# A retention layer with two GLU-like blocks: raw weight pieces requested two conversions ahead, q scaled one slot earlier, the second stage's first inputs loaded and split in the first

## Chip, core and metric

One core of one Trainium2 chip. The metric is device time in microseconds (us) for one launch of the whole computation; lower is better. The engines are TensorE (PE, matmuls; PEld is its weight load), VectorE (DVE), ScalarE (ACT), GpSimd (POOL) and the queue that issues DMAs, SyncE (SP). Each engine runs its own list of instructions in order.

## What is computed

```python
# q, k, v: 8 batches, 8 heads, 576 positions, 64 per head
scores = 1/sqrt(64) * q @ k.T                      # per batch and head
ret    = scores * D        # D[i, j] = gamma_h ** (i - j) where i >= j, else 0
x      = (ret @ v), heads side by side             # 4608 x 512
h      = ((x @ w1) * (x @ w2)) @ w3                # 512 -> 1024 -> 1024
y      = h @ w_out                                 # 1024 -> 512
u      = y @ w2_in                                 # 512 -> 2048
out    = (u - tanh(u)) @ w2_out                    # 2048 -> 512
```

The six weights arrive as 64-bit floats (the kernel sees them as 64-bit integers) and are split on the chip into a high and a low 32-bit part; every large product is made of three matmuls, high*high, low*high and high*low.

## The kernel before

**Tiles.** The 4608 rows are cut into 12 tiles of 384. The work is in three stages that follow each other on TensorE.

**First stage.** A *unit* (t, m) is 24 matmuls of 384 columns: `half_s(t, m, 0)` makes 128 columns of x@w1, `half_s(t, m, 1)` those of x@w2, each into its own PSUM buffer (`psab`, pool `psm`, four buffers, so two units). `finish()` of the next unit copies the first to `a` on ScalarE (L423), multiplies it with the second on VectorE into `pf` (L425), and has the product stored to DRAM (`pdr`). There are 96 units, 0 to 95. The list `units` fixes their order; the loop at L583 writes the program unit by unit, and all other work of the stage is emitted at fixed places inside that loop:

- **Retention by chunks.** x comes from 40 chunks (up to 128 positions of one batch). For the first ten (`chunk_at`, units 0 to 10, the *head*) q is scaled on VectorE (`attn_scale`, L232, together with the scaling of v on ScalarE, L216), q and k are transposed on TensorE (`attn_1`, L243) and copied, `attn_2` makes the scores (`pss`, L260) and masks them (`pt`), `attn_3` makes the outputs, and `attn_x` splits them into `x`. The other thirty run as `stages`: q and k are loaded in small pieces (`load_qk` puts 32 of them for two chunks on the list `pend`, and `trickle` issues ten at each unit, L296), GpSimd scales q, VectorE transposes.
- **Conversions.** `Conv` turns one 512 KB piece of weights into 32-bit halves: `load` issues the DMA of `raw` (L136), `a` reads it on ScalarE (L142, `cf`), `b` is four VectorE operations, `c` writes the high part on ScalarE (L159), `d` the low part on VectorE. A `Queue` runs jobs in steps: an even step does `b` of job j and loads job j+`ahead`; an odd step does `a` of job j+1 and `c`, `d` of job j. In the head the queue of w1 and w2 has `ahead=3`.
- **Side work.** From unit 16 on the generator `side_s` is advanced at the start of each unit, 95 steps spread evenly over the units (1.2 per unit). It converts w_out and w3 (`ahead=1`, two `raw` buffers), transposes w3 (`w34_t`, `pst`, L464), multiplies w3 by w_out (`w34_p`, `psw`), reloads the eight products `w34` from DRAM (L509), and converts the second half of w2_out.

**Second stage.** y = p @ w34, 48 steps of 24 matmuls (`psy`); `p_load` brings `pin` from `pdr`, `p_split` splits it (L679, L680). The pool of `pin` and `p` is opened after the first stage's pools are closed, at L642, and the first loads and splits stand at L697 to L700. The remaining conversions run beside it.

**Third stage.** h (`psh`), the gate on ScalarE and VectorE, and the last product (`psout`).

The SP queue issues in program order, so a load stands behind everything emitted before it.

Of the kernel before, what the change touches and what calls it, by code (L numbers as in the profile page):

```python
# [28 lines left out]
def retention_glu_tanh_kernel(  # L29
# [66 lines left out]
    tp = sl_.enter_context(tc.tile_pool(name="tp", bufs=2, reuse_waits="tile"))  # L96
    ap_ = sl_.enter_context(tc.tile_pool(name="attn", bufs=1, reuse_waits="tile"))
    cv_ = ExitStack()
# [25 lines left out]
    class Conv:  # L124
# [5 lines left out]
        def load(self):  # L130
            self.pool, bufs = (hv, 4) if self.pool == "head" else (cv, 2)
            self.raw = self.pool.tile([P, 512], I64, name="raw", bufs=bufs)
            dst = self.raw
            if len(self.src.shape) == 3:
                dst = dst.rearrange("p (k m) -> p k m", k=self.src.shape[1])
            SP.dma_start(out=dst, in_=self.src)  # L136
# [7 lines left out]
        def b(self):  # L144
            self.t = self.pool.tile([P, 512], F32, name="ct")
            fu, tu = self.f.bitcast(U32), self.t.bitcast(U32)
            DVE.tensor_scalar(tu, self.hi, 0x80000000, None, op0=ALU.bitwise_and)
            DVE.scalar_tensor_tensor(fu, fu, 3, tu, op0=ALU.logical_shift_left, op1=ALU.bitwise_or)
            DVE.tensor_scalar(tu, fu, 0xFF800000, None, op0=ALU.bitwise_and)
            DVE.scalar_tensor_tensor(self.t, self.lo, 2.0**-52, self.t, op0=ALU.mult, op1=ALU.mult)  # L150
# [266 lines left out]
    def finish():  # L417

        if not open_:
            return  # L420
        t, m, pss = open_.pop()
        a = tp.tile([P, T], F32, name="a")
        ACT.activation(a, pss[0][:, :T], AF.Copy)  # L423
        pf = tp.tile([P, T], F32, name="pf", bufs=3)
        DVE.tensor_tensor(pf, a, pss[1][:, :T], op=ALU.mult)  # L425
        later(SP, pdr[t][:, m], pf, 1)
        if m == FF - 1:
            del xt[t]
# [51 lines left out]
    def side_s():  # L480

        jobs = [Conv(w_out[f * P:f * P + P, :], target=wo_target(f)) for f in range(FF)]

        jobs += [Conv(w3[r * P:r * P + P, g * 512:g * 512 + 512], full=True, target=w3_target(r, g))
                 for r in range(FF) for g in range(2)]
        qu = Queue(jobs)
        qu.start()
        yield
        for n in range(len(jobs)):
            qu.step()  # L490
            yield
            qu.step()
            yield
            if n >= FF:
                r, g = divmod(n - FF, 2)
                w34_t(r, g)
                yield
                if g == 1:
                    w34_p(r)
                    yield  # L500

        for _ in range(4):
            yield
        wg_.close()
        w34p = w34_.enter_context(tc.tile_pool(name="w34p", bufs=1, side="right", reuse_waits="tile"))
        w34.extend(w34p.tile([P, 2, DM], F32R, name=f"w34_{i}") for i in range(FF))
        lp[0] = lp_.enter_context(tc.tile_pool(name="lp", bufs=2, side="right", reuse_waits="tile"))
        for f in range(FF):
            SP.dma_start(out=w34[f].rearrange("p t n -> p (t n)").bitcast(F32), in_=wdr34[f])  # L509
        qu = Queue([Conv(w2_out[f * P:f * P + P, :], store=wdr_out[f - NR]) for f in range(NR, FF2)])  # L510
        qu.start()
        yield
        while qu.step():
            yield
        for _ in range(2):
            yield

# [52 lines left out]
    for i in range(NH, len(chunks)):  # L570
        p = int(14.0 + 2.28 * (i - NH))
        stages += [(p - 1, stage_q, (i,)), (p, stage_0, (i,)), (p + 1, stage_1, (i,)), (p + 2, attn_4, (i,))]
    stages.sort(key=lambda e: e[0])

    TRK = 10
    SIDE = 95
    sn = 0
    si = 0
    side = None
    wg_ = ExitStack()  # L580
    w34_ = ExitStack()
    w34 = []
    for n, (t, m) in enumerate(units):  # L583
        if n == N0:
# [6 lines left out]
            side = side_s()  # L591
        while side is not None and sn < (n - N0 + 1) * SIDE / (len(units) - N0 - 1):
            sn += 1
            if next(side, 1) == 1:
                side = None
# [3 lines left out]
        if i is not None and i > 2:  # L599
# [4 lines left out]
            if i + 1 < NH:  # L604
                attn_2(i + 1, sap)
            if i + 2 < NH:
                attn_scale(i + 2)
        want = conv_at[n] if n < len(conv_at) else 0
# [5 lines left out]
        if i is not None and i + 2 < NH:  # L614
            attn_1(i + 2)
        while q12.n < want:
            q12.step()
# [5 lines left out]
        if n == 13:  # L623
            load_qk(next_pair(NH))
        while si < len(stages) and stages[si][0] <= n:
            stages[si][1](*stages[si][2])
            si += 1
# [8 lines left out]
    w2r = ctx.enter_context(tc.tile_pool(name="w2r", bufs=1, reuse_waits="tile"))  # L636
    w2o = {f: w2r.tile([P, 2, DM], F32R, name=f"w2o{f}") for f in range(NR)}
    yrp = ctx.enter_context(tc.tile_pool(name="yr", bufs=1, reuse_waits="tile"))
    ys_ = ExitStack()
    ysp = ys_.enter_context(tc.tile_pool(name="ysp", bufs=1, reuse_waits="tile"))  # L640
    pp_ = ExitStack()
    pp = pp_.enter_context(tc.tile_pool(name="pp", bufs=3, side="right", reuse_waits="tile"))  # L642
    w2i = {}

    def w2i_target(f):
        def g(j):
            if f % 2 == 0:
                w2i[f // 2] = slot(f // 2, f"w2i{f // 2}")
            s = w2i[f // 2][:, (f % 2) * 1024:(f % 2) * 1024 + 1024]
            j.high, j.low = s[:, :512], s[:, 512:]  # L650
        return g

    def w2o_target(f):
        def g(j):
            j.high, j.low = w2o[f][:, 0, :], w2o[f][:, 1, :]
        return g

    jobs = []
    for f in range(FF2):
        jobs.append(Conv(w2_in[:, f * P:f * P + P].rearrange("(k p) c -> p k c", p=P), target=w2i_target(f)))  # L660
        if f < NR:
            jobs.append(Conv(w2_out[f * P:f * P + P, :], target=w2o_target(f)))
    q2 = Queue(jobs)
    q2.start()

    pin = {}
    pq = {}
    py = [(t, f) for t in range(NTL) for f in range(0, FF, 2)]

    def p_load(n):  # L670
        if n < len(py):
            t, f = py[n]
            pin[n] = pp.tile([P, 2, T], F32, name="pin")
            SP.dma_start(out=pin[n], in_=pdr[t][:, f:f + 2])

    def p_split(n):
        if n < len(py):
            g = pp.tile([P, 2, 2, T], F32R, name="p")
            ACT.activation(g[:, 0], pin[n], AF.Copy)  # L679
            DVE.tensor_tensor(g[:, 1], pin.pop(n), g[:, 0].bitcast(F32), op=ALU.subtract)  # L680
            pq[n] = g

    def y_load(t):
# [12 lines left out]

    for n in range(3):  # L697
        p_load(n)
    p_split(0)
    p_split(1)  # L700
    acc = {}

# [176 lines left out]
```

## Time and profile before

| | |
|---|---|
| median of 3 runs | 1688.05 us (1687.34 to 1690.17) |
| the profiled execution, its own time | 1687.88 us |
| its span, first to last instruction | 1686.1 us |
| mean granted TensorE clock | 0.983 |
| PE busy | 1616.0 us (96%) |
| DVE busy | 1118.5 us (66%) |
| ACT busy | 868.4 us (52%) |
| DMA | 157.95 MB, 94 GB/s over the span |

Busy time counts an engine's instructions as they run; a busy TensorE is not always at its full clock, so the granted clock is read beside it. What a change is worth is read from the places where TensorE stands idle, and from what it was waiting for there.

### The profile page before, as it was taken

The numbers are of one execution on the slowest core, as the hardware profiler recorded it, in microseconds if no ns is written. First come the engines' busy times: TensorE is split into PE (matmuls) and PEld (weight loads), VectorE is DVE, ScalarE is ACT, GpSimd is POOL, SyncE is SP. The second block draws the span as 40 slices with busy tenths as digits, with TensorE's granted clock in tenths as the row PEclk, the third lists the DMA queues.
The fourth block names the chain that finished last, engine by engine and source line by source line (L and its number), as shares of the span: only waits on it lengthen the run. The fifth ranks groups of instructions, "written<-read, shape, count | busy, mean of one in ns | idle before, by whom it ended". The sixth has DMA issues, their size and how long they took to land.

```text
span 1686.1 us, 26796 instructions
## 1 busy us (share of the span) xinstructions
PE 1616.0 (96%) x10128; PEld 1502.7 (89%) x10128; DVE 1118.5 (66%) x2006; ACT 868.4 (52%) x1929; POOL 30.0 (2%) x35
## 2 busy tenths in 40 slices
PE   6798979999999999899999999999999999999999
PEld 5798878988899989899999999999999999999998
DVE  5963645544444454666748777777887877777776
ACT  5532323222223222344437777777776677777775
POOL 0000000000000000000000000000000000000000
PEclk8999989999999999899999999999999999999999
DMA  9625455554554473666643000100010000001000
GB/s 200 168 81 130 117 129 134 130 133 113 132 138 108 114 255 129 216 223 204 215 130 141 20 19 20 38 19 20 19 38 20 19 29 29 19 20 38 1 20 19
DMA packets 261249, 157.95 MB, mean 94 GB/s; under 512 B 209152, under 2 KB 238080, under 8 KB 261120
## 3 DMA queue, kind: packets, MB, share of 16 engines
q1 hardware_dynamic: 259392, 146.81, 31.8%
q10 hardware_dynamic: 1728, 9.44, 1.3%
q8 instruction: 79, 1.29, 0.3%
q14 instruction: 50, 0.41, 0.1%
HBM read 110.05 MB, written 46.14 MB: 93 GB/s over the span
## 4 chain that ended last, share of the span: by engine, by line
PE 84%; SPq 5%; DVE 5%; DMA 4%; issue 1%; ACT 1%; DVEq 0%; ACTq 0%
PE psh L122 8%; PE psh L120 8%; PE psh L121 8%; PE psout L122 8%; PE psout L120 8%; PE psout L121 8%; PE psab L120 6%; PE psab L122 5%; PE psab L121 5%; PE psy L120 4%; PE psy L122 4%; PE psy L121 4%; SPq L296 4%; DMA raw<-in_moe_w_out_dram 2%; PE pss L260 1%; PE pso L364 1%
## 5 line engine op out<-in xcount | busy, mean ns | idle before, releaser
L120 PE MATMUL psab<-x,w 128*128 128x384 f32 x768 | 269.4, 351 | 26.9 <-ACT a L423 26.9
L122 PE MATMUL psab<-x,w 128*128 128x384 f32 x768 | 262.0, 341 | 0.0
L121 PE MATMUL psab<-x,w 128*128 128x384 f32 x768 | 261.8, 341 | 0.0
L122 PE MATMUL psh<-yhl,w2i 128*128 128x384 f32 x768 | 258.9, 337 | 0.0
L120 PE MATMUL psh<-yhl,w2i 128*128 128x384 f32 x768 | 258.1, 336 | 0.0
L121 PE MATMUL psh<-yhl,w2i 128*128 128x384 f32 x768 | 257.9, 336 | 0.0
L122 PE MATMUL psout<-w2o,g 128*128 128x512 f32 x576 | 227.0, 394 | 0.0
L120 PE MATMUL psout<-w2o,g 128*128 128x512 f32 x576 | 226.8, 394 | 0.0
L121 PE MATMUL psout<-w2o,g 128*128 128x512 f32 x576 | 225.4, 391 | 0.0
L768 ACT ACTIVATE u<-psh 128x384 f32<-128x384 f32 x192 | 94.4, 492 | 222.2 <-PE psh L122 222.1
L120 PEld LDWEIGHTS psab<-x,w 128*128 128x128 f32 x768 | 148.1, 193 | 32.7 <-ACT a L423 28.1
L776 DVE TENSOR_TENSOR w<-u,psh 128x384 f32<-128x384 f32 x192 | 106.0, 552 | 82.2 <-ACT th L770 82.0
L789 DVE TENSOR_TENSOR g<-w,g 128x384 fp32r<-128x384 f32 x192 | 107.0, 557 | 69.9 <-ACT g L788 69.8
L121 PEld LDWEIGHTS psh<-yhl,w2i 128*128 128x128 f32 x768 | 144.3, 188 | 8.5
L120 PEld LDWEIGHTS psh<-yhl,w2i 128*128 128x128 f32 x768 | 144.3, 188 | 8.1
L121 PEld LDWEIGHTS psab<-x,w 128*128 128x128 f32 x768 | 148.3, 193 | 0.4
L122 PEld LDWEIGHTS psab<-x,w 128*128 128x128 f32 x768 | 147.9, 193 | 0.4 <-DVE x L396 0.4
L122 PEld LDWEIGHTS psh<-yhl,w2i 128*128 128x128 f32 x768 | 144.2, 188 | 0.0
L120 PE MATMUL psy<-p,w 128*128 128x384 f32 x384 | 129.4, 337 | 7.1 <-ACT p L679 7.1
L122 PEld LDWEIGHTS psout<-w2o,g 128*128 128x128 f32 x576 | 108.0, 188 | 25.6
L122 PE MATMUL psy<-p,w 128*128 128x384 f32 x384 | 129.3, 337 | 0.0
L121 PE MATMUL psy<-p,w 128*128 128x384 f32 x384 | 129.2, 336 | 0.0
(85 smaller groups left out, 2742.5 us busy)
## 6 DMA issues: line engine op xcount, KB each, us to landing
pdr<-pf SPq DMA_DIRECT2D x96, 192.0 KB, 2.9
pin<-pdr SPq DMA_DIRECT2D x48, 384.0 KB, 4.1
raw<-in_moe_w_dram SPq DMA_DIRECT2D x32, 512.0 KB, 5.0
raw<-in_moe_w_out_dram SPq DMA_DIRECT2D x24, 512.0 KB, 4.2
ydr<-ys ACTq DMA_DIRECT2D x12, 768.0 KB, 5.8
yin<-ydr SPq DMA_DIRECT2D x12, 768.0 KB, 4.2
out_dram<-os SPq DMA_DIRECT2D x36, 256.0 KB, 2.2
kn<-in_k_dram SPq DMA_DIRECT2D x32, 256.0 KB, 3.1
```

What stands on the lines that cost most here:

```text
L120: PE.matmul(ps, lh, rh, start=first, stop=False)
L121: PE.matmul(ps, ll, rh, start=False, stop=False)
L122: PE.matmul(ps, lh, rl, start=False, stop=last)
L260: PE.matmul(pss[e][:n, j, :n], kT[r:r + D, j, :n], qT[r:r + D, j, :n], start=True, stop=True)
L296: SP.dma_start(out=o, in_=i_)
L364: PE.matmul(po[D * e:D * e + D, j, :n], vn[:n, 2 * j + e, :], pt[:n, j, e, :n], start=(c == 0 and j == 0), stop=(j == NP - 1), skip_group_ ...
L768: ACT.activation(u, h, AF.Square)
L776: DVE.tensor_tensor(w, u, h, op=ALU.mult)
L789: DVE.tensor_tensor(g[:, 1, :], w, g[:, 0, :].bitcast(F32), op=ALU.subtract)
```

## The change

Five things are done. (1) The queues of the side work and of the second stage load two jobs ahead instead of one; `raw` gets a third buffer, and to make room `ct` and `a` get one buffer instead of two. (2) The side generator is split: `side_s` ends with the reload of `w34`, and a new `side_o` converts the second half of w2_out from unit 84 on, two steps per unit; inside `side_s` the transposes of w3 are emitted one step later, and its 79-step budget spreads the steps at 1.18 per unit. (3) In the head `attn_scale` is called for chunk i+3 behind `attn_1(i+2)`, instead of for chunk i+2 in front of it. (4) At unit 84 the retention pool is closed and the pool of `pin` and `p` opened; the first three `pin` are loaded at unit 91, two of them split at unit 94, where the second stage's queue is started too. (5) The retention stages are spaced by 2.26 units instead of 2.28.

```diff
         def load(self):
-            self.pool, bufs = (hv, 4) if self.pool == "head" else (cv, 2)
+            self.pool, bufs = (hv, 4) if self.pool == "head" else (cv, 3)
...
         def b(self):
-            self.t = self.pool.tile([P, 512], F32, name="ct")
+            self.t = self.pool.tile([P, 512], F32, name="ct", bufs=1)
...
-        a = tp.tile([P, T], F32, name="a")
+        a = tp.tile([P, T], F32, name="a", bufs=1)
...
-        qu = Queue(jobs)
+        qu = Queue(jobs, ahead=2)
         qu.start()
         yield
-        for n in range(len(jobs)):
+        yield
+        for n in range(len(jobs) + 1):
             qu.step()
             yield
+            if n > FF:
+                w34_t(*divmod(n - FF - 1, 2))
             qu.step()
             yield
-            if n >= FF:
-                r, g = divmod(n - FF, 2)
-                w34_t(r, g)
+            if n > FF and (n - FF) % 2 == 0:
+                w34_p((n - FF) // 2 - 1)
                 yield
-                if g == 1:
-                    w34_p(r)
-                    yield
...
-        qu = Queue([Conv(w2_out[f * P:f * P + P, :], store=wdr_out[f - NR]) for f in range(NR, FF2)])
+    def side_o():
+
+        qu = Queue([Conv(w2_out[f * P:f * P + P, :], store=wdr_out[f - NR]) for f in range(NR, FF2)], ahead=2)
         qu.start()
         yield
         while qu.step():
             yield
-        for _ in range(2):
-            yield
...
-        p = int(14.0 + 2.28 * (i - NH))
+        p = int(14.0 + 2.26 * (i - NH))
...
-    SIDE = 95
+    NO = 84
...
-        while side is not None and sn < (n - N0 + 1) * SIDE / (len(units) - N0 - 1):
+        if n == NO:
+            assert side is None and si == len(stages) and not pend
+            at_.close()
+            pp = pp_.enter_context(tc.tile_pool(name="pp", bufs=3, side="right", reuse_waits="tile"))
+            lp[0] = lp_.enter_context(tc.tile_pool(name="lp", bufs=2, side="right", reuse_waits="tile"))
+            side, sn = side_o(), 0
+        n0, n1, steps = (N0, NO - 1, 79) if n < NO else (NO, len(units) - 3, 18)
+        while side is not None and sn < (n - n0 + 1) * steps / (n1 - n0):
...
             if i + 1 < NH:
                 attn_2(i + 1, sap)
-            if i + 2 < NH:
-                attn_scale(i + 2)
...
         if i is not None and i + 2 < NH:
             attn_1(i + 2)
+            if i + 3 < NH:
+                attn_scale(i + 3)
...
+        if n == len(units) - 5:
+            for e in range(3):
+                p_load(e)
+        if n == len(units) - 2:
+            q2.start()
+            p_split(0)
+            p_split(1)
...
-    q2 = Queue(jobs)
-    q2.start()
+    q2 = Queue(jobs, ahead=2)
...
-    for n in range(3):
-        p_load(n)
-    p_split(0)
-    p_split(1)
```

VectorE's program in the head, from the second conversion of unit 2 to the product of unit 2 (`w_3` is the weight of unit 3, `qn` the q of a chunk); before, then as changed:

```order
L147 TENSOR_SCALAR ct<-raw 128x512
L148 SCALAR_TENSOR_TENSOR cf<-cf,ct 128x512
L149 TENSOR_SCALAR ct<-cf 128x512
L150 SCALAR_TENSOR_TENSOR ct<-raw,ct 128x512
L165 TENSOR_TENSOR cf<-cf,w_3_710 128x512
L166 TENSOR_TENSOR w_3_710<-cf,ct 128x512
L380 COPY state<-psu 64x4x64 x2
L396 TENSOR_TENSOR x<-pso,x 128x4x128
L262 TENSOR_TENSOR pt<-pss,cst 128x4x128 x2
L232 TENSOR_TENSOR qn<-qn,dec 128x512
L425 TENSOR_TENSOR pf<-a,psab 128x384
```

```order
L148 TENSOR_SCALAR ct<-raw 128x512
L149 SCALAR_TENSOR_TENSOR cf<-cf,ct 128x512
L150 TENSOR_SCALAR ct<-cf 128x512
L151 SCALAR_TENSOR_TENSOR ct<-raw,ct 128x512
L233 TENSOR_TENSOR qn<-qn,dec 128x512
L166 TENSOR_TENSOR cf<-cf,w_3_710 128x512
L167 TENSOR_TENSOR w_3_710<-cf,ct 128x512
L381 COPY state<-psu 64x4x64 x2
L397 TENSOR_TENSOR x<-pso,x 128x4x128
L263 TENSOR_TENSOR pt<-pss,cst 128x4x128 x2
L426 TENSOR_TENSOR pf<-a,psab 128x384
```

The same chunk's q is scaled in front of the second weight's low part, and no longer between the mask `pt` and `pf`; nothing is added.

The SP queue around the raw piece of w_out's seventh job (`raw`; `pdr` rows mark the units 23 and 24, `kb` and `qb` are the small pieces of k and q); before, then as changed:

```order
L115 DMA pdr_71<-pf 128x384
L296 DMA kb<-in_k_dram 32x8x32 x10
L115 DMA pdr_71<-pf 128x384
L296 DMA kb<-in_k_dram 32x8x32 x2
L296 DMA qb<-in_q_dram 32x8x32 x8
L312 DMA kn<-in_k_dram 128x8x64
L312 DMA vn<-in_v_dram 128x8x64
L136 DMA raw<-in_moe_w_out_dram 128x512
```

```order
L116 DMA pdr_71<-pf 128x384
L297 DMA kb<-in_k_dram 32x8x32 x10
L137 DMA raw<-in_moe_w_out_dram 128x512
L116 DMA pdr_71<-pf 128x384
L297 DMA kb<-in_k_dram 32x8x32 x2
L297 DMA qb<-in_q_dram 32x8x32 x8
L313 DMA kn<-in_k_dram 128x8x64
L313 DMA vn<-in_v_dram 128x8x64
```

The piece moves up by one unit, past ten small pieces, a k and a v. ScalarE's program around the first reading of that piece (the `cf` in front of `wo_1611`; each `a` marks a unit, `vn` is the scaling of v); before, then as changed:

```order
L423 ACTIVATE a<-psab 128x384
L216 ACTIVATE vn<-vn,dec 64x64 x8
L142 ACTIVATE cf<-raw 128x512
L159 ACTIVATE wo_1611<-cf 128x512
L423 ACTIVATE a<-psab 128x384
```

```order
L217 ACTIVATE vn<-vn,dec 64x64 x8
L143 ACTIVATE cf<-raw 128x512
L160 ACTIVATE wo_1610<-cf 128x512
L424 ACTIVATE a<-psab 128x384
L396 ACTIVATE x<-pso 128x4x64
L424 ACTIVATE a<-psab 128x384
L217 ACTIVATE vn<-vn,dec 128x64 x8
L143 ACTIVATE cf<-raw 128x512
L160 ACTIVATE wo_1611<-cf 128x512
L424 ACTIVATE a<-psab 128x384
```

The reading stands two units later, so that load and reading are three units apart; before, both were emitted at the start of unit 25.

SP's program at the end of the first stage (`pin` is the second stage's input, `wdo<-hl` the stored halves of w2_out); before, then as changed:

```order
L115 DMA pdr_80<-pf 128x384 x2
L115 DMA wdo_108<-hl 128x1024
L115 DMA pdr_80<-pf 128x384 x4
L136 DMA raw<-in_moe_w_in_dram 128x4x128
L674 DMA pin<-pdr_69 128x768 x4
```

```order
L116 DMA pdr_80<-pf 128x384
L549 DMA pin<-pdr_69 128x768 x3
L116 DMA wdo_107<-hl 128x1024
L116 DMA pdr_80<-pf 128x384
L116 DMA wdo_108<-hl 128x1024
L116 DMA pdr_80<-pf 128x384 x2
L137 DMA raw<-in_moe_w_in_dram 128x4x128
L137 DMA raw<-in_moe_w_out_dram 128x512
L116 DMA pdr_80<-pf 128x384 x3
L549 DMA pin<-pdr_69 128x768
```

Three of the first four inputs are asked for ahead of the last seven stores instead of behind them.

## Rows read from the trace of the kernel before

**Rows 1.** Waits of TensorE, whole span: waited for, us in total, times, longest.

```profile
PE psab L120 <- ACT a L423: 26.9, 6, 10.6
PE psq L243 <- DVE qn L232: 19.9, 7, 5.9
PE psy L120 <- ACT p L679: 7.1, 1, 7.1
PE pst L464 <- DVE w3f L163: 6.5, 3, 3.4
```

**Rows 2.** Timeline of TensorE, head: start, length, operation, [idle before, releaser].

```profile
5.90 1.12 PE L243 MATMUL psq<-cst,qn 128*128 128x128 f32 x4 [5.90 <-DVE qn L232]
...
31.46 1.09 PE L243 MATMUL psq<-cst,qn 128*128 128x128 f32 x4 [4.83 <-DVE qn L232]
...
87.01 0.34 PE L120 MATMUL psab<-x,w 128*128 128x384 f32 x1
```

**Rows 3.** Windows, head: stretch, length, busy PE, PEld, DVE, ACT, POOL, clock, DMA.

```profile
60.00:70.00 10.00, 8.04 (x80) 7.31 (x80) 9.68 (x18) 6.26 (x16) 0.00 (x0) 1.00 0.83 191
```

**Rows 4.** Timeline of VectorE, end of the head's conversions.

```profile
77.73 0.69 DVE L166 TENSOR_TENSOR w<-cf,ct 128x512 fp32r<-128x512 f32 x1
...
80.09 0.42 DVE L396 TENSOR_TENSOR x<-pso,x 128x256 fp32r<-128x256 f32 x1 [0.45 <-ACT x L395]
...
81.63 0.68 DVE L232 TENSOR_TENSOR qn<-qn,dec 128x512 f32<-128x512 f32 x1
```

**Rows 5.** Chain that ended last, 200 to 240 us: start, length, what.

```profile
214.22 0.45 SPq L296
214.71 0.45 SPq L312
...
215.88 6.62 DMA raw<-in_moe_w_out_dram
...
224.20 0.69 PE psab L120
```

**Rows 6.** Windows, TensorE only, behind stalls: stretch, length, busy (matmuls), clock, DMA.

```profile
83.28:87.00 3.72, 3.72 (x15) 0.54 0.16 57
155.40:159.40 4.00, 3.99 (x15) 0.62 0.43 97
185.00:189.00 4.00, 3.99 (x14) 0.59 0.41 163
224.20:230.20 6.00, 6.00 (x19) 0.51 0.67 165
...
352.30:356.30 4.00, 4.00 (x18) 0.59 0.60 143
...
462.30:466.30 4.00, 4.00 (x16) 0.58 0.43 68
605.10:609.10 4.00, 3.94 (x14) 0.57 0.30 67
678.70:686.70 8.00, 7.92 (x30) 0.66 0.66 217
690.00:700.00 10.00, 10.00 (x59) 1.00 0.56 161
```

**Rows 7.** DMA issues: what, count, KB each, median us to landing.

```profile
raw<-in_moe_w_out_dram SPq DMA_DIRECT2D x24, 512.0 KB, 4.2
...
w<-wd SPq DMA_DIRECT2D x8, 512.0 KB, 7.0
```

**Rows 8.** Line L296: operation, ns min/median/max, first and last start.

```profile
L296 SPq DMA_DIRECT2D qb<-in_q_dram x288: 311/448/2344, 119.0 to 567.2; - x144
L296 SPq DMA_DIRECT2D kb<-in_k_dram x288: 311/448/1855, 127.6 to 579.3; - x144
```

**Rows 9.** Timeline of ScalarE, quiet units.

```profile
131.94 0.49 ACT L423 ACTIVATE a<-psab 128x384 f32<-128x384 f32 x1 [3.67 <-PE psab L122]
```

**Rows 10.** Timeline of VectorE, same stretch.

```profile
129.92 0.55 DVE L425 TENSOR_TENSOR pf<-a,psab 128x384 f32<-128x384 f32 x1 [3.61 <-PE psab L122]
```

More of the change, by code (lines that the diff above doesn't have):

```diff
@@ L96, in retention_glu_tanh_kernel @@
     tp = sl_.enter_context(tc.tile_pool(name="tp", bufs=2, reuse_waits="tile"))
-    ap_ = sl_.enter_context(tc.tile_pool(name="attn", bufs=1, reuse_waits="tile"))
+    at_ = ExitStack()
+    ap_ = at_.enter_context(tc.tile_pool(name="attn", bufs=1, reuse_waits="tile"))
     cv_ = ExitStack()
@@ L514, in side_s, with w2i_target, g, w2o_target @@
             yield
-        for _ in range(2):
-            yield
+    w2i = {}
+    w2o = {}
+    def w2i_target(f):
+        def g(j):
+            if f % 2 == 0:
+                w2i[f // 2] = slot(f // 2, f"w2i{f // 2}")
+            s = w2i[f // 2][:, (f % 2) * 1024:(f % 2) * 1024 + 1024]
+            j.high, j.low = s[:, :512], s[:, 512:]
+        return g
+    def w2o_target(f):
+        def g(j):
+            j.high, j.low = w2o[f][:, 0, :], w2o[f][:, 1, :]
+        return g
+    jobs = []
+    for f in range(FF2):
+        jobs.append(Conv(w2_in[:, f * P:f * P + P].rearrange("(k p) c -> p k c", p=P), target=w2i_target(f)))
+        if f < NR:
+            jobs.append(Conv(w2_out[f * P:f * P + P, :], target=w2o_target(f)))
+    q2 = Queue(jobs, ahead=2)
+    pin = {}
+    pq = {}
+    py = [(t, f) for t in range(NTL) for f in range(0, FF, 2)]
+    def p_load(n):
+        if n < len(py):
+            t, f = py[n]
+            pin[n] = pp.tile([P, 2, T], F32, name="pin")
+            SP.dma_start(out=pin[n], in_=pdr[t][:, f:f + 2])
+    def p_split(n):
+        if n < len(py):
+            g = pp.tile([P, 2, 2, T], F32R, name="p")
+            ACT.activation(g[:, 0], pin[n], AF.Copy)
+            DVE.tensor_tensor(g[:, 1], pin.pop(n), g[:, 0].bitcast(F32), op=ALU.subtract)
+            pq[n] = g
     NH = 2 * NA
@@ L575, in retention_glu_tanh_kernel @@
     TRK = 10
-    SIDE = 95
+    NO = 84
+    side_n = {}
     sn = 0
@@ L581, in retention_glu_tanh_kernel @@
     w34_ = ExitStack()
+    pp_ = ExitStack()
     w34 = []
@@ L636, in retention_glu_tanh_kernel @@
     w2r = ctx.enter_context(tc.tile_pool(name="w2r", bufs=1, reuse_waits="tile"))
-    w2o = {f: w2r.tile([P, 2, DM], F32R, name=f"w2o{f}") for f in range(NR)}
+    w2o.update((f, w2r.tile([P, 2, DM], F32R, name=f"w2o{f}")) for f in range(NR))
     yrp = ctx.enter_context(tc.tile_pool(name="yr", bufs=1, reuse_waits="tile"))
@@ L640, in retention_glu_tanh_kernel @@
     ysp = ys_.enter_context(tc.tile_pool(name="ysp", bufs=1, reuse_waits="tile"))
[L641 to L662, printed above, removed]
-    q2 = Queue(jobs)
-    q2.start()
[L666 to L681, printed above, removed]
     def y_load(t):
```

1 line of the change is left out of this document (removed).

## The prediction

> **What bounds the kernel now.** The profiled execution took 1687.88 us, 0.17 us under the median of the runs; its span is 1686.1 us, so 1.8 us lie around it. TensorE is busy for 1616.0 us of it, so I first asked where it stands idle. The list of TensorE's waits [rows 1] holds nearly all of the missing 70 us, in four groups, and all of them lie in the first 679 us: 26.9 us in six waits of a unit's first matmul for the copy `a` (its PSUM buffer is not free), 19.9 us in seven waits of `psq` for the scaled q, 6.5 us in three waits of w3's transpose for `w3f`, and one wait of 7.1 us at the start of the second stage.
>
> What stands behind `a` is read from the chain around the longest of these waits [rows 5]. SP issues its small q and k pieces one after another, about 0.49 us apart (214.22 to 214.71), and only then, at 215.88, the raw weight piece; that lands 6.6 us later. ScalarE had the reading of that piece in front of the copy `a`, so TensorE starts again at 224.20. The wait is not ScalarE's work but a load asked for too late: in the program of before, this piece is loaded and read at the start of the same unit.
>
> A stall costs more than its length. Behind it the rows of windows [rows 6] show the granted clock at 0.51 to 0.66, that is partly at 1.2 instead of 2.4 GHz, while the undisturbed stretch has 1.00 and 59 matmuls in 10.00 us, 0.1695 us each. Taking each window's busy time less its matmuls at 0.1695 us: 1.2 us behind the head's last wait (3.72 less 15 x 0.1695), then 1.45, 1.6, 2.8, 0.95, 1.3 and 1.6 us behind six side stalls, 9.7 together, and 2.8 us (7.92 less 30 x 0.1695) behind the wait between the stages.
>
> **The change part by part.** *Raw pieces two ahead.* At stake are 26.9 + 6.5 = 33.4 us of waits [rows 1] and 9.7 us of slow clock [rows 6], 43.1 us. In the program of before, some pieces are loaded and read at the start of the same unit, as the seventh of w_out is; with two ahead that one has three units between, and the order gives every piece at least one, nearly all two to four. A unit is 24 matmuls, at least 24 x 0.1695 = 4.1 us, so two units are 8.1 us and more with the retention work. The late piece above cost 10.6 us of wait; it now is asked for one unit earlier and read two units later, 12 us at least, which covers it. No instruction is added: the same loads are issued by SP at another place, past ten small pieces that now wait 0.45 us more. The three transposes are emitted a step later, when `w3f` is a step old, so their 6.5 us go too.
>
> What stays: the very first piece has only one unit, behind the long run of small pieces that SP has to issue for the first chunks; I leave 1.5 us there. SP itself gets less time: it issues 576 small pieces between 119.0 and 579.3 us [rows 8], at 0.49 us 282 us, and some 170 other loads and stores at about 0.45 us, 76 us, so it is busy for 358 of 460 us, 78%. If TensorE gets through the same stretch 43 us faster, that is 86%, and where there is no w3 work yet the small pieces come in denser runs; I leave 2 us for a piece that is late there. The reload of `w34` moves from unit 79 to unit 70, among the last q and k pieces: eight pieces of 512 KB with a median landing of 7.0 us [rows 7]; I leave 1.5 us (bounds: nothing, if the pieces behind it are as early as the order says, to 10 us, a landing and the rest of a unit). With these 5 us the side work brings 38 us. Bounds: 43 us, and half of it, 21 us, if SP takes back as much as it is given.
>
> *Single buffers.* `ct` is written and read by VectorE alone, in order, so one buffer adds no wait. For `a` ScalarE must now wait until `pf` of the unit before has read it. In a quiet unit `pf` ends at 130.47 [rows 10] and the next `a` starts at 131.94 [rows 9], 1.5 us later. I take nothing; the price if VectorE falls behind is a rival below.
>
> *q a slot earlier.* Of the 19.9 us [rows 1] the waits of 5.90 and 4.83 us [rows 2] belong to chunks whose scaling is not moved; 9.2 us in five waits and the 1.2 us of slow clock are at stake. But the head is VectorE's: 9.68 of 10 us busy [rows 3]. The scaling is only put elsewhere in its program, so the same sum of VectorE's work still lies in front of TensorE, and the waits for q turn in part into waits for the weights' low parts. What is won is the end of that run: the second product of unit 4 needs a weight that VectorE finishes at 78.4 (77.73 + 0.69), and unit 5 needs the split x that it finishes at 80.5 (80.09 + 0.42) [rows 4]. Unit 5 begins at 87.01 now [rows 2], behind the q of 81.63 [rows 4] and the slow stretch. With one more scaling of 0.6 us in front it can begin at 81.2. That gives 5.8 us, and 0.2 for the last small wait: 6 us. The bounds are nothing (VectorE's sum decides all) and 10.4 us. ScalarE's 2 us of scaling v move along; ScalarE is 63% busy there and has the time.
>
> *The stage border.* The loads of `pin` and their splits now lie in units 91 and 94, so the first `psy` finds its input ready: 7.1 + 2.8 = 9.9 us. Its cover is five units of 4.1 us, 20 us, against waits of 7 us now; the reloaded `w34` has long landed, and the PSUM buffers of the first products are those of the finished retention. What it costs: two splits of VectorE more in unit 94, and in units 84 to 92 the conversions at one job per unit, six operations of 0.4 to 0.7 us and the product's 0.5, which nearly fill VectorE's 4.1 us. Were the splits late by half, 5 us would be left of the gain; I take all of it.
>
> The sum is 38 + 6 + 9.9 = 53.9 us off 1687.88: **1634 us**.
>
> **The rivals.** *SP is the bound of the first stage.* Around the longest stall SP issues without a pause [rows 5], and if pieces are asked for earlier it has nothing to give: the q and k pieces come late in place of the raw ones, VectorE waits for them and TensorE for VectorE. Against it: 78% over the stretch, and the raw pieces that had one unit or more between load and use show no stall behind them. Half of the 43.1 us would stay: 1687.9 less (21.5 + 6 + 9.9) gives 1650 us. [...]
>
> *The head gains nothing.* VectorE's 9.68 of 10 us speak for it, the work that lies behind its last conversion against it. That is 1634 + 6 = 1640 us.
>
> *The reload of w34 among the q and k pieces* blocks SP long enough for one stall: 10 us and 1.5 of slow clock instead of my 1.5, 1644 us.
>
> *Slower.* The single `a` ties ScalarE to VectorE. To eat 54 us and 3.4 more (0.2%), `a` would have to make TensorE lose 0.7 us in each of the 80 units from 16 to 95, so `pf` would have to be later by the slack of 1.5 us and that, 2.2 us in every unit, and at the same time the second PSUM buffer's two units of slack would have to be used up. The first happens only behind conversions. At 0.8 us a unit it would be 1634 + 64 = 1698 us.
>
> *The change does not do what it says:* the raw pieces come no earlier because SP is held up in front of them in any case, and the border finds a new wait of the same size; within 3 us of 1688.
>
> **How the numbers follow.** Forecast 0.66, with 1625 to 1645 as its own range; SP-bound 0.17 (1645 to 1660); no gain in the head 0.09; the reload 0.04; slower 0.02; no effect 0.02. For 8 in 10 the range runs from 1624, where all 63 us are won (43.1 + 10.4 + 9.9), to 1652, which takes in the SP-bound case's centre. A measurement of this kernel can tell 0.2%, 3.4 us, from no change; all cases but the last two are faster than that: 0.96 faster, 0.02 same, 0.02 slower.
>
> **What would show it.** In the waits of TensorE, the line of `a` falls from 26.9 to under 5 us and the transposes' line vanishes; the waits of ScalarE's `cf` for raw pieces shrink with it. The head's waits for q are gone, shorter ones for `w` stand there, and unit 5 begins near 81 us. The first `psy` follows the last `psab` without a gap. If instead VectorE's transposes wait for `kb` or `qb` around units 18 to 28, SP was the bound; if TensorE waits around unit 72, it was the reload. The first `psy` stands at 678.8 us now (671.7 and the wait of 7.1) and should stand at 628 (38 + 6 + 7.1 earlier); later than 633 means that the side work brought less than I count. The third stage should not move at all; a difference there would mean that something other than these waits decides.

## Result and the profile after

The changed kernel takes 1646.03 us (median of 4 runs, 1644.32 to 1649.17) against 1689.11 us (1687.34 to 1690.24, 4 runs) in the same comparison: a ratio of 0.9748 with an interval of 0.9729 to 0.9767, 43 us less. The forecast was 1634 with 1624 to 1652: the time lies in the range, 12 us above the forecast. It lies just past the 1625 to 1645 that the prediction kept for its own account, where its stretch for SP as the bound begins. The profiled execution took 1644.32 us; its span is 1642.5 us at a mean granted clock of 0.995, and TensorE is busy for 1607.4 us of it.

First the waits of TensorE in the changed kernel, as in [rows 1]: waited for, us in total, times, longest.

```profile
PE psq L244 <- DVE qn L233: 10.9, 3, 5.7
PE pss L261 <- DVE qT L346: 5.0, 2, 4.5
PE psq L244 <- DVE state L381: 4.7, 2, 2.6
...
PE psab L121 <- DVE pf L426: 3.0, 1, 3.0
PE psk L244 <- DVE x L397: 1.6, 2, 0.9
PE pso L365 <- ACT vn L217: 1.4, 1, 1.4
PE psq L244 <- DVE state L383: 0.7, 2, 0.4
```

The lines of `a`, of `w3f` and of `psy` are gone, and q's 19.9 us in seven waits are 10.9 in three; two of those are the chunks that the forecast had left out. In their place stand lines that were not at stake: the scores wait for `qT`, the outputs for `vn`, a product's first matmul for `pf`, and q's and k's transposes for `state` and `x`. The kernel before waited for `state` as well, in a line that [rows 1] does not show:

```profile
PE psq L243 <- DVE state L380: 2.0, 1, 2.0
```

These waits have grown to 5.4 us. A line for the first chunk's `kT`, 4.0 us, is the same before and after.

The border comes out as forecast. In TensorE's timeline the first `psy` follows the last `psab` without a gap:

```profile
637.74 0.34 PE L123 MATMUL psab<-x,w 128*128 128x384 f32 x1
637.92 0.33 PE L121 MATMUL psy<-p,w 128*128 128x384 f32 x1
```

The windows of the changed kernel (stretch, length, busy PE, PEld, DVE, ACT, POOL, clock, DMA) answer to [rows 3] and [rows 6]: the head, the stretches behind its longest wait and behind the two long waits of the side work, and the start of the second stage.

```profile
60.00:70.00 10.00, 7.30 (x75) 6.26 (x74) 9.65 (x18) 6.11 (x16) 0.00 (x0) 0.99 0.85 187
69.60:73.00 3.40, 3.40 (x14) 3.40 (x13) 3.30 (x7) 1.04 (x3) 0.00 (x0) 0.53 0.30 80
...
207.00:211.00 4.00, 4.00 (x17) 3.93 (x16) 2.47 (x5) 0.36 (x2) 0.00 (x0) 0.65 0.83 194
219.60:225.60 6.00, 6.00 (x34) 5.44 (x35) 5.33 (x10) 2.38 (x10) 0.00 (x0) 0.72 0.89 224
637.90:645.90 8.00, 8.00 (x48) 8.00 (x47) 7.09 (x12) 1.94 (x3) 0.00 (x0) 1.00 0.78 270
```

The second stage now starts at the full clock (1.00, before 0.66). VectorE still fills the head (9.65 of 10 us). Behind three waits the clock falls as it did before, to 0.53, 0.65 and 0.72 of 2.4 GHz, so partly to 1.2.

Where the 43.6 us between the two profiled executions were won is read from the starts of the units. Up to unit 11, 3.8 us (of which unit 0 already has 0.8; its start lies between 35.8 and 37.8 us in the kernels here, whatever the edit, so from unit 0 to unit 11 it is 3.0: 83.5 us before, 80.5 after); from unit 11 to unit 84, 30.2 us; from unit 84 to the first `psy` 6.9, and 2.7 us of slow clock behind it. The forecast was 6 for the head, 38 for the side work and 9.9 for the border.

**What was late in the side work.** TensorE's two long waits there, in its timeline:

```profile
205.67 1.47 PE L261 MATMUL pss<-qT,kT 64*128 64x128 f32 x16 [4.51 <-DVE qT L346]
...
219.56 0.45 PE L121 MATMUL psab<-x,w 128*128 128x384 f32 x1 [3.03 <-DVE pf L426]
```

Two more follow in units 73 and 74 (0.43 us for `qT` and 1.35 for `vn`). With the slow clock behind the two long ones (some 1.3 and 1.5 us; behind the other two the granted clock stays at 1.00) this makes 12.1 us where the forecast left 5. What stands behind them is seen in SP's timeline of the changed kernel, with the count of issues at the end of a row:

```profile
194.15 4.92 SPq L297 DMA_DIRECT2D kb<-in_k_dram  x10
199.16 0.39 SPq L137 DMA_DIRECT2D raw<-in_moe_w_out_dram  x1
199.66 0.38 SPq L116 DMA_DIRECT2D pdr<-pf  x1
200.08 1.03 SPq L297 DMA_DIRECT2D kb<-in_k_dram  x2
201.21 3.92 SPq L297 DMA_DIRECT2D qb<-in_q_dram  x8
205.17 0.45 SPq L313 DMA_DIRECT2D kn<-in_k_dram  x1
205.74 0.52 SPq L313 DMA_DIRECT2D vn<-in_v_dram  x1
206.35 0.97 SPq L116 DMA_DIRECT2D pdr<-pf  x1
207.37 4.88 SPq L297 DMA_DIRECT2D qb<-in_q_dram  x8
212.29 0.94 SPq L297 DMA_DIRECT2D kb<-in_k_dram  x2
213.33 0.39 SPq L137 DMA_DIRECT2D raw<-in_moe_w_out_dram  x1
```

SP issues almost without a pause for 19 us (its own waits between 194 and 214 us come to 1.0 us). The raw piece of [rows 5], which was asked for at 215.88 behind kn and vn, is asked for at 199.16 here. But what stands behind the small pieces is still late, and it is other loads now: the q pieces, v, and the stores of `pf`. VectorE's timeline shows the stores and the q pieces:

```profile
192.10 0.56 DVE L426 TENSOR_TENSOR pf<-a,psab 128x384 f32<-128x384 f32 x1 [3.72 <-DMA pdr<-pf]
...
204.31 0.71 DVE L344 STREAM_TRANSPOSE kT<-kb 128x512 f32<-128x512 f32 x1 [6.61 <-DMA qb<-in_q_dram]
...
213.78 0.69 DVE L166 TENSOR_TENSOR cf<-cf,wo 128x512 f32<-128x512 f32 x1 [4.28 <-ACT wo L160]
```

The wait of 3.72 us for a store reaches no wait of TensorE. Only a later one does, 6.18 us at 526.23 behind the reload of `w34`: VectorE works without a pause from there to the transposes that TensorE finds 0.43 us late. ScalarE's list of waits shows v beside the raw pieces, before and then after:

```profile
ACT cf L142 <- DMA raw<-in_moe_w_out_dram: 60.9, 11, 15.8
...
ACT cf L142 <- DMA raw<-in_moe_w_dram: 22.4, 5, 9.7
...
ACT vn L216 <- DMA vn<-in_v_dram: 3.0, 1, 3.0
```

```profile
ACT vn L217 <- DMA vn<-in_v_dram: 50.3, 11, 13.0
...
ACT cf L143 <- DMA raw<-in_moe_w_out_dram: 13.5, 6, 4.1
...
ACT cf L143 <- DMA raw<-in_moe_w_dram: 3.7, 1, 3.7
```

ScalarE's waits for raw pieces fell from 83 us to 17, as they were meant to; its waits for v rose from 3.0 to 50.3 us. Most of that is hidden. One wait, of 13.0 us, is not: it ends at 210.64, 4.9 us after SP asked for v at 205.74. Behind v's scaling ScalarE has the reading of a raw piece that has landed by then (no wait stands in front of it), and its high part `wo`. VectorE stands idle for that one for 4.28 us (the row at 213.78); its next `pf` comes behind it and a further conversion, at 218.96, and TensorE's wait of 3.03 us at 219.56 is for that `pf`.

### The profile page after: what moved, and what is told of

It is laid out like the page before. It is cut to its first block, busy times and chain, and to the rows that moved or that the text cites. A ratio compares the mean times of both kernels' runs of the same rounds, so it can differ in the third digit from the quotient of the medians.

```text
span 1642.5 us, 26852 instructions
## 1 busy us (share of the span) xinstructions
PE 1607.4 (98%) x10128; PEld 1493.0 (91%) x10128; DVE 1119.7 (68%) x2006; ACT 869.6 (53%) x1929; POOL 31.7 (2%) x35
## 4 chain that ended last, share of the span: by engine, by line
PE 87%; DVE 5%; DMA 4%; SPq 3%; ACT 1%; issue 1%; DVEq 0%; ACTq 0%
PE psh L123 8%; PE psh L121 8%; PE psh L122 8%; PE psout L123 8%; PE psout L121 8%; PE psout L122 8%; PE psab L121 6%; PE psab L123 5%; PE psab L122 5%; PE psy L123 4%; PE psy L122 4%; PE psy L121 4%; SPq L297 2%; PE pso L365 2%; PE pss L261 2%; PE pso L359 1%
## 5 line engine op out<-in xcount | busy, mean ns | idle before, releaser
L121 PE MATMUL psab<-x,w 128*128 128x384 f32 x768 | 266.0, 346 | 3.2 <-DVE pf L426 3.0
L123 PE MATMUL psab<-x,w 128*128 128x384 f32 x768 | 259.0, 337 | 0.1
L122 PE MATMUL psab<-x,w 128*128 128x384 f32 x768 | 258.8, 337 | 0.0
L786 DVE TENSOR_TENSOR w<-u,psh 128x384 f32<-128x384 f32 x192 | 106.2, 553 | 80.9 <-ACT th L780 80.5
L121 PEld LDWEIGHTS psab<-x,w 128*128 128x128 f32 x768 | 145.4, 189 | 9.1 <-DVE pf L426 4.0
L122 PEld LDWEIGHTS psab<-x,w 128*128 128x128 f32 x768 | 145.7, 190 | 0.4
L123 PEld LDWEIGHTS psab<-x,w 128*128 128x128 f32 x768 | 145.6, 190 | 0.4 <-DVE x L397 0.4
L793 DVE COPY_PREDICATED w<-u,th 128x384 f32<-128x384 int32 x192 | 116.0, 604 | 20.9 <-DVE w L792 1.4
L123 PE MATMUL psy<-p,w 128*128 128x384 f32 x384 | 128.3, 334 | 0.0
L121 PE MATMUL psy<-p,w 128*128 128x384 f32 x384 | 128.3, 334 | 0.0
```

The costliest lines, as they stand in the source:

```text
L121: PE.matmul(ps, lh, rh, start=first, stop=False)
L122: PE.matmul(ps, ll, rh, start=False, stop=False)
L123: PE.matmul(ps, lh, rl, start=False, stop=last)
L786: DVE.tensor_tensor(w, u, h, op=ALU.mult)
L793: DVE.copy_predicated(w, u.bitcast(I32), th)
```

## Experiments

Each kernel was timed beside the kernel before, whose median lay between 1689.3 and 1690.2 us. All but e7 start from the changed kernel.

**e1: the old place of the scaling.**

```diff
+            if i + 2 < NH:
+                attn_scale(i + 2)
         want = conv_at[n] if n < len(conv_at) else 0
...
-            if i + 3 < NH:
-                attn_scale(i + 3)
```

> The changed kernel with the scaling of q put back in front of its transposes in the head; all else stays. Theory: the head is bound by VectorE's sum of work and by the PSUM buffers that its state and x operations free, so the earlier scaling won only the 3.5 us by which unit 5 starts sooner (83.5 against 87.0): unit 5 back near 87, time near 1649.5. Rival A, the forecast's 6 us, with the rest lost elsewhere: 1652. Rival B, the later work of the first stage takes up any head start: no change, 1646.

1650.79 us (1649.86 to 1653.32), ratio 0.9776 (0.9759 to 0.9793): 4.8 us slower than the changed kernel by the medians, with intervals that just overlap; in the profile unit 11 starts 2.6 us later. In its list of TensorE's waits the old line is back:

```profile
PE psq L244 <- DVE qn L233: 19.1, 7, 6.1
```

So the moved scaling is not nothing, and it is not the 9.0 us by which the q waits shrink. Its size in the head is read from unit 0 to unit 11: 82.5 us here, 80.5 in the changed kernel; 83.5 in the kernel before and 82.7 in e7, which have the old place too. That is 2 to 3 us. The profiled executions lose another 3.1 us between unit 11 and the first `psy`, where the two programs are the same; what makes these is not shown.

**e2: loads one ahead again.**

```diff
-        qu = Queue(jobs, ahead=2)
+        qu = Queue(jobs, ahead=1)
```

> The changed kernel with the side work's queue loading one job ahead again (three buffers and the single ones stay). Theory: the loads' lead is what removed the six waits for the copy of a unit's first product; they come back where load and reading are at the start of one unit, with most of the 26.9 us and the slow clock behind them: 1665 to 1680, and ScalarE waits for raw pieces 50 us and more. Rival: the new step rate and the later transposes did it and the lead little: under 1652.

1662.92 us (1660.72 to 1664.65), ratio 0.9843 (0.9822 to 0.9864): 16.9 us slower. The waits for `a` return:

```profile
PE psab L121 <- ACT a L424: 10.8, 6, 6.5
PE psw L121 <- ACT a L424: 8.8, 3, 4.2
```

The waits of `psab` are shorter than the 26.9 us of before, and three waits of `psw` are new. Undoing the lead in loading costs some 17 of the 30 us; the other edits of the generator are undone in e9.

**e3: the border put back.** The three loads, two splits and the start of the second stage's queue stand behind the first stage again.

```diff
-        if n == len(units) - 5:
-            for e in range(3):
-                p_load(e)
-        if n == len(units) - 2:
-            q2.start()
-            p_split(0)
-            p_split(1)
...
+    q2.start()
+    for n in range(3):
+        p_load(n)
+    p_split(0)
+    p_split(1)
     acc = {}
```

> The changed kernel with the second stage's first loads and splits put back behind the first stage (its pools stay opened at unit 84). Theory: the whole 7.1 us of wait and 2.7 us of slow clock return: 1656, first matmul of the second stage 7 us behind the last of the first. Rival: with the pool open earlier the loads need not wait for the first stage's buffers, and SP is free by then, so they run ahead and half or less returns: 1647 to 1651.

1658.97 us (1656.77 to 1660.98), ratio 0.9822 (0.9803 to 0.984): 12.9 us slower. The wait is back in TensorE's timeline, 1.8 us longer than in [rows 1], with 2.8 us of slow clock behind it:

```profile
648.52 0.69 PE L121 MATMUL psy<-p,w 128*128 128x384 f32 x1 [8.86 <-ACT p L554]
```

**e4: the first q and k pieces, and with them the first whole k and v, four units earlier.**

```diff
-        if n == 10:
+        if n == 6:
             load_qk(NH)
             load_kv(NH)
-        if n == 13:
+        if n == 9:
             load_qk(next_pair(NH))
```

> The changed kernel with the first two groups of small q and k pieces put on the list at units 6 and 9 instead of 10 and 13, nothing else. Theory: SP's queue, busy without a pause from about 190 to 213 us, is what makes the q and k pieces and a v late at units 25 to 28 (TensorE waits 4.5 and 3.0 us there, and 2.9 us of slow clock follow); four units' start brings it 20 us ahead, the waits go, 1637 to 1640. Rival A: what is late is the data of the DMA engines and not SP's issuing: no change within 2 us. Rival B: the early pieces collide with the head's weight loads and VectorE's conversions wait: slower, 1648 to 1655.

1639.99 us (1639.1 to 1642.57), ratio 0.9712 (0.9695 to 0.9729): 6 us faster than the changed kernel by the medians, though the two profiled executions are only 1.8 us apart. The wait at 205.67 goes; unit 30 starts 27.3 us before its place in the kernel before, and only 19.2 in the changed one. The wait of unit 28 for `pf` stays, a little shorter:

```profile
212.50 0.44 PE L121 MATMUL psab<-x,w 128*128 128x384 f32 x1 [2.63 <-DVE pf L426]
```

Two more waits, 2.36 us for `a` at 248 and 1.91 for v at 534, are longer than anything in their places in the changed kernel. So one wait went, and others stayed or grew: it is not all of the 12 us. What made the two late is not traced here.

**e5: the reload of w34 at unit 77.**

```diff
-        for _ in range(4):
+        for _ in range(13):
             yield
```

> As the changed kernel, but the side generator idles 13 steps instead of 4 in front of the reload of w34, so that its eight 512 KB loads are asked for around unit 77 instead of unit 70, behind the last q and k pieces. My theory: the reload cost 0.4 + 1.4 us of waits around unit 72 (scores, and outputs waiting for v) and some 0.3 us of slow clock; these two waits go and the time is 2 us lower, 1644, which this measurement can just not tell from no change. Rival, the reload's price is the 10 us that I named: 1636. If the time rises, the reload is now too late for the second stage, and the first psy waits for w.

1643.68 us (1639.62 to 1644.45), ratio 0.9718 (0.9699 to 0.9738). The waits in units 73 and 74 are gone, and the first `psy` stands 1.2 us earlier. This fits the 2 us that I named; by the medians alone, 2.4 us, it can just not be told from no change. The 10 us of the rival are excluded.

**e6: k, v and the raw pieces from ScalarE's queue**, those of the head's weights excepted.

```diff
-            SP.dma_start(out=dst, in_=self.src)
+            (SP if self.pool is hv else ACT).dma_start(out=dst, in_=self.src)
...
-            SP.dma_start(out=t[:n], in_=src[b, s0:s0 + n])
+            ACT.dma_start(out=t[:n], in_=src[b, s0:s0 + n])
```

> As the changed kernel, but the whole k and v of the thirty later chunks (60 loads) and the raw weight pieces of the side work and the second stage are issued from ScalarE's queue, not from SP. Theory, SP's own issuing is the limit around units 25 to 28: SP is relieved of 60 + 60 issues of 0.45 us in the first stage, v no longer comes 13 us late, and the waits of 4.5 us (scores for qT) and 3.0 us (psab behind pf) shrink: 1636 to 1641. Rival, what was late there is the transfer itself, the DMA engines or DRAM: no change, 1646. Second rival, ScalarE pays for the issues with its own time and stands behind pieces whose buffer is not free: ScalarE's copy a is late again, 1650 or more.

1636.24 us (1635.7 to 1637.84), ratio 0.9681 (0.9664 to 0.9697): 9.8 us faster. The same bytes come from the same places; only who asks for them has changed. This speaks for the asking as what was late, and not the transfer; e10 shows the landing times.

**e7: the kernel before with one buffer for `a` and `ct`.**

```diff
-            self.t = self.pool.tile([P, 512], F32, name="ct")
+            self.t = self.pool.tile([P, 512], F32, name="ct", bufs=1)
...
-        a = tp.tile([P, T], F32, name="a")
+        a = tp.tile([P, T], F32, name="a", bufs=1)
```

> The kernel before with one thing alone: a and ct have one buffer instead of two. My theory: the price of the single buffers is nothing, 1689, within 2 us of the kernel before. The rival of the prediction (ScalarE tied to VectorE) at a smaller size: some of the 12 us that the changed kernel falls short come from it, 1692 to 1700 here, with TensorE's waits for a longer than 26.9 us.

1690.6 us (1685.43 to 1694.54, 10 runs), ratio 1.0001 (0.9987 to 1.0015). The single buffers cost nothing there. TensorE's waits for `a` stay at 27.0 us in six waits, against the 26.9 of [rows 1].

**e8: the low part behind `state` and `x`.** In the head, the `d` of each w2 piece waits for the next slot's `attn_x`.

```diff
                 self.jobs[j].c()
-                self.jobs[j].d()
+                if self is q12 and j % 2:
+                    last.append(self.jobs[j])
+                else:
+                    self.jobs[j].d()
...
+    def low():
+        while last:
+            last.pop(0).d()
...
                 attn_load(i + 4)
+            low()
             if i + 1 < NH:
                 attn_2(i + 1, sap)
+        low()
```

> As the changed kernel, but in the head the low part of each w2 piece (two operations of VectorE, 1.4 us) is emitted behind the next slot's state and x instead of in front of them. Theory: psq and psk wait for PSUM buffers that state and x have to free, 0.34 + 0.95 + 2.60 + 0.36 + 0.61 us in the changed kernel and 1.6 us of slow clock behind the longest; with state and x 1.4 us earlier most of it goes, unit 5 begins 1 to 2 us before 83.5 and the time is 1643 to 1645. Rival, VectorE's sum of work in front of unit 5 decides: the waits move to psab for w, unit 5 stays within 0.5 us of 83.5 and the time at 1646. If TensorE's second product needs the low part at once, unit 5 is later than 83.5.

1649.84 us (1647.38 to 1651.35), ratio 0.9758 (0.974 to 0.9777): 3.8 us slower than the changed kernel by the medians, with intervals that overlap; in the profile unit 5 starts at 85.1 instead of 83.5. The wait for `state` at unit 3's transposes is halved (2.60 to 1.27 us), but TensorE now finds the weight missing, as its timeline shows just where the forecast had its last step:

```profile
80.42 0.66 PE L254 MATMUL psk<-cst,kn 128*128 128x128 f32 x4 [0.61 <-DVE x L407]
81.75 0.69 PE L122 MATMUL psab<-x,w 128*128 128x384 f32 x1 [0.49 <-DVE w L167]
```

My expectation was wrong, and the rival's is right in kind: moved back, the low part is late itself, and with 1.5 us of slow clock behind 81.75 more is lost than won. In size it is the last sentence of what I expected that came true: unit 5 is later than 83.5. This fits an account in which VectorE's sum decides, and does not prove it.

**e9: w3's transposes directly behind their conversion.** The generator has its old steps again, and with them one idle step at its start instead of two and a later reload of `w34`.

```diff
         yield
-        yield
-        for n in range(len(jobs) + 1):
+        for n in range(len(jobs)):
             qu.step()
             yield
-            if n > FF:
-                w34_t(*divmod(n - FF - 1, 2))
             qu.step()
             yield
-            if n > FF and (n - FF) % 2 == 0:
-                w34_p((n - FF) // 2 - 1)
+            if n >= FF:
+                r, g = divmod(n - FF, 2)
+                w34_t(r, g)
                 yield
+                if g == 1:
+                    w34_p(r)
+                    yield
```

> As the changed kernel, but w3's transposes stand again directly behind the conversion of their piece and have a step of their own, as before; the load stays two ahead. This also moves the reload of w34 to about unit 81. Theory, which counted the transposes' line as a part of its own: the 6.5 us of waits for w3f return, with some 3 us of slow clock behind them, less 2 us that the later reload gives: 1652 to 1656. Rival, the wait for w3f was only the late raw piece seen through the conversion, so that the lead in loading is enough: 1644 to 1646.

1657.11 us (1654.28 to 1659.45), ratio 0.9803 (0.9787 to 0.982): 11.1 us slower. The waits for `w3f` return in full although the loads are two ahead, so they were never a late load seen through the conversion. The wait of 5.3 us in the line of `a` is another matter: it stands at 150.19 us, at the first raw piece, which the dropped idle step has left with less time.

```profile
PE pst L465 <- DVE w3f L164: 8.2, 4, 3.5
PE psab L121 <- ACT a L424: 6.5, 3, 5.3
```

**e10: only k and v from ScalarE's queue** (the second half of e6's edit).

> As the changed kernel, but only the 60 loads of whole k and v go from ScalarE's queue; the raw weight pieces stay on SP. It parts the 9.8 us that both together gave. If the lateness of v and of qT around units 25 to 28 is SP's dense run of issues, 60 of the 120 issues give about half: 1640 to 1642, with v's wait of 13 us gone and a rest of the wait for pf or for a left. If the raw pieces were the part that counted, 1645; if k and v were all of it, 1636.

1637.5 us (1636.4 to 1638.3), ratio 0.9687 (0.967 to 0.9703): 8.5 us faster. This is below my 1640 to 1642; nearly all of e6's gain is k and v. In ScalarE's timeline v is asked for at 194.06, not at 205.74, and is scaled at 198.13 without a wait:

```profile
194.06 0.41 ACTq L313 DMA_DIRECT2D vn<-in_v_dram  x1
...
198.13 2.01 ACT L217 ACTIVATE vn<-vn,dec 128x64 f32<-128x64 f32 x8
```

The transfers did not get shorter. From asking to landing the thirty k and v took, least, median and most, in the changed kernel and then in e10:

```profile
DMA to landing us min/median/max: 2.6/3.4/5.0
DMA to landing us min/median/max: 2.7/3.6/6.9
```

So for v what was late was the asking. ScalarE's waits for v fall from 50.3 to 2.1 us. The longest of the side work's waits that is left is the 3.00 us for `qT` at 204.77, with q's last pieces late as before; 1.49 us for `pf` at 288 and 0.77 for `w3f` at 284 are new.

**e11: e4 and e6 together.**

> As the changed kernel, with k, v and raw pieces on ScalarE's queue and the first q and k pieces four units earlier. If both act on the same thing, SP's dense stretch around units 25 to 28, they do not add: 1634 to 1637. If they were separate gains, 6 and 9.8 us add to 1630.

1631.34 us (1630.43 to 1634.6), ratio 0.9655 (0.964 to 0.9671): 14.7 us faster than the changed kernel. The two add, nearly (6 and 9.8), against my theory. Put on top of e6, e4's edit gives 4.9 us by the medians and 5.3 by the profiled executions. TensorE's list for e6 alone still has 2.2 us for `qT` at 141 and 1.1 for `a` at 242; both are gone here, and between units 16 and 84 no wait is longer than 0.5 us.

**e12: e11 with the late reload of e5.**

> As the run before, and the reload of w34 moved from unit 70 to 77. Relieved of 120 issues, SP has time for the reload where it stands, so the change is within 1 us: 1633 to 1637. All of the side work's waits should be gone, and the first psy stand at 628 to 630, the place that the prediction had given it.

1629.73 us (1628.99 to 1630.2), ratio 0.9642 (0.9627 to 0.9656), the fastest of all, and faster than I expected; the first `psy` stands at 623.8, before the 628 to 630. To e11 it is 1.6 us, and the two profiled executions have the first `psy` within 0.3 us, so the reload adds nothing that can be told. Its list of TensorE's waits has nothing long left behind the head:

```profile
PE pss L261 <- DVE qT L346: 0.5, 1, 0.5
PE psab L121 <- DVE pf L426: 0.2, 1, 0.2
```

From unit 11 to unit 84 it gains 43.9 us on the kernel before.

## Why the prediction came out as it did

Between the profiled executions the forecast is 10 us too high: 8 of them are the side work and 2 the head. (The profiled execution of the changed kernel is the fastest of its four, 1.7 us under their median, which makes the 12.)

**The side work: the stake was right, what stays was too small.** The forecast put 43.1 us at stake and left 5. When SP is relieved (e12), 43.9 us come back, so 33.4 us of waits and 9.7 of slow clock behind them were the right size. In the changed kernel 30.2 came, and the step that failed is "with these 5 us the side work brings 38 us":

- The first raw piece: 1.5 us left, nothing lost. The second idle step at the generator's start gives it its time; without it e9 loses 5.3 us there.
- A late piece where SP is dense: 2 us left, 10.3 measured (4.51, 3.03 and the slow clock behind them). This is the failing term. From 78% for SP's whole stretch I drew that SP has time; but the queue is in order, and in units 25 to 27 it has none. The mean itself was a little low: SP's own waits in the kernel before come to 79 of the 460 us, so it issued for 83%, and in the changed kernel 53 of 442, 88%. And the trace of before already showed the dense part: between 119 and 222 us SP waited for 12 of 103 us only. A raw piece that is asked for earlier lands earlier, and q and v behind the same small pieces are what TensorE waits for instead. The rival that SP is the bound named this sign (transposes that wait for `qb`), and it did come, at a quarter of the 43.1 us and not at half. e6 and e10 show the cause: asked for by another queue, and so earlier, the same loads take 8 to 10 us off, with transfers that are no shorter; e4 agrees, with less weight.
- The reload: 1.5 us left, 1.8 measured (0.43 and 1.35); e5 agrees.

The Trainium skill ("Perfetto Trace Analysis", section "What 'DMA-bound' means") lists, among the things that a DMA-bound kernel can be bound on, the sequencer of the issuing engine, whose track is then solid with DMA slices. The trace agrees for 194 to 213 us, where SP's track is solid; there, moving loads only changed which of them was late. The stage as a whole is not bound so: SP waits for 53 of its 442 us, and loads moved earlier took 17 us off (e2).

The two halves of the side work are separate, as the forecast counted them: the load's lead is 17 us (e2), the transposes a step later together with the second idle step 11 (e9). These are the prices of undoing one edit in the new kernel, and need not add up to the 30.

**The head: 6 forecast, 3.0 in the profile from unit 0 to unit 11 (3.8 with the earlier start of unit 0).** Undoing the move (e1) gives 1.9 of the 3.0 back. The argument (VectorE's sum decides, what is won is the end of the run) fits, e8 included. The step that failed is "with one more scaling of 0.6 us in front it can begin at 81.2". VectorE was on time: `x` ends at 80.85. But TensorE had more to do behind it than the forecast let it. Its timeline:

```profile
79.67 0.63 PE L244 MATMUL psq<-cst,qn 128*128 128x128 f32 x4 [0.36 <-DVE state L383]
80.91 0.66 PE L244 MATMUL psk<-cst,kn 128*128 128x128 f32 x4 [0.61 <-DVE x L397]
81.32 0.42 PE L121 MATMUL psab<-x,w 128*128 128x384 f32 x1
...
83.51 0.33 PE L121 MATMUL psab<-x,w 128*128 128x384 f32 x1
```

and VectorE's in front of it:

```profile
78.06 0.69 DVE L167 TENSOR_TENSOR w<-cf,ct 128x512 fp32r<-128x512 f32 x1
78.67 0.85 DVE L383 TENSOR_TENSOR state<-psu,state 64x256 f32<-64x256 f32 x2
...
80.43 0.42 DVE L397 TENSOR_TENSOR x<-pso,x 128x256 fp32r<-128x256 f32 x1 [0.45 <-ACT x L396]
```

The weight is ready at 78.75, yet unit 4's second product starts at 81.32: in TensorE's program k's transposes stand in front of it, and they wait for a PSUM buffer that `x` frees. Then come its own 12 matmuls, 2.2 us, to 83.5. The forecast had `x` and the weight as conditions of unit 5 side by side; in truth the product of the one stands behind the wait for the other. Unit 5 begins at 83.5 and not at 81.2, and the 2.3 us between are this product.

The waits for q did turn into others, but not into waits for `w`, as I had written: TensorE waits for `state` and `x`, whose PSUM buffers the transposes want. The 2.60 us of the longest then cost 1.6 us of slow clock as well (0.53 in the windows).

**The border: 9.9 forecast, 9.6 in the profile.** 7.1 us of wait and 2.7 of slow clock are gone, and 0.4 us are lost again in units 84 to 95. That is not VectorE's new work there: in e6, e9, e11 and e12, which have the same work, these units take 49.75 us, as in the kernel before. Undoing it costs 12.9 (e3), more than it brought: with two loads ahead, two raw pieces of the second stage stand in front of the first `pin` and not one, so it is asked for 2.5 us behind the first stage's last matmul (before 1.9), and its split starts 5.8 us later (before 4.6).

**The single buffers: nothing,** by e7, where the change's other parts are away; in the changed kernel ScalarE does wait for `pf` in front of `a` (13.1 us in 11 waits), but TensorE's line of waits for `a` is gone all the same.

**The third stage does not move,** as forecast: from the first `psy` to the end of the span it is 1004.6 us after and 1007.3 before, and the difference is the 2.7 us of slow clock at the start of the second stage.

## What to carry to other kernels

A queue's mean load says little about what moving a load within it will bring: read the issuing queue, in the trace of before, where the stall is, and if it issues without a pause there, count the loads behind the one that is moved, for one of them will be the next late one; start the burst earlier or give some of it to another queue. A stake that is summed from waits and the slow clock behind them came out here (43.1 us counted, 43.9 won back in e12); the part that is won needs the next condition on the same engine, and an engine's program order can turn two conditions that look parallel into one after the other. Where two engines hand buffers to each other in a saturated stretch, as in the head, moving an operation forward made others later, so look at the end of the run. And measure a stretch from its own start: the start of unit 0 shifted by up to 2 us from kernel to kernel here.

## What the runs showed of the hardware

What SP pays for a load does not grow with its size here. In the rows of its timeline the issue of a raw piece of 512 KB takes 0.39 us, that of a whole v of 256 KB 0.52 us, and the eight q pieces of 32 KB at 201.21 take 3.92 us, 0.49 us each. So a tile that is cut into 32 pieces costs the queue about what 32 large loads would, and the loads behind it pay. On ScalarE's queue in e10 an issue of v took 0.37 to 0.89 us, 0.59 in the median, and with the 60 issues there TensorE had one wait of 0.4 us for `a`.
